# Chunked attention with 64 keys per 32 queries: no mask, a pair of heads in one tile, in front of two MoE layers

## The chip, the core and the metric

The kernel runs on one core of a Trainium2 chip. The metric is the device time of one execution in microseconds (us), as the median of several runs.

## The reference, cut to what matters

```python
batch, n_heads, seq, head_dim, n_mem = 2, 8, 768, 64, 8
chunk, left_ctx, right_ctx = 32, 16, 8
for c in range(seq // chunk):                      # 24 chunks of 32 queries
    l, r = max(0, c*chunk - left_ctx), min(seq, (c+1)*chunk + right_ctx)
    k_full = concat([mem_k, k[:, :, l:r]]); v_full = concat([mem_v, v[:, :, l:r]])   # 8 + up to 56 keys
    a = exp(scores - max(scores)); a = a / (sum(a) + 1e-9)       # scores = q_c @ k_full.T / 8
    out[:, :, c*chunk:(c+1)*chunk] = a @ v_full
x = out as (B, S, 512)
x = sigmoid(xr @ w_r) * (relu(xk @ w_k)**2 @ w_v)  # xk, xr: each row mixed with the row before it
# then: every row goes to one of 8 experts (sticky choice), out = p * (relu(x @ w1[e]) @ w2[e])
```

So each chunk of 32 queries sees at most 8 + 16 + 32 + 8 = 64 keys.

## The kernel before

**Stages.** The 1536 rows are four units of 384 (UT). For a unit, attention runs in 4 pairs of heads, 16 pairs n in all. Its output xT goes through the mixing (`mix_d`, `mix_a`, `mix_hi`, `mix_lo`) into 20 blocks of matmuls per unit: 8 for k (`k_mm`), 4 for r (`r_mm`), 8 halves for v (`v_mm`); a block is 4 triples, and a triple is the three fp32r matmuls of `mm3` (high by high, high by low, low by high part; lines 514 to 516). `v_out` (line 573) ends an output tile. Routing follows (`route_l`, `route_a`, `route_y`, `route_b`, `route_c`), and after the fourth unit come slots of 128 rows for one expert each (`slot_body`) and half slots of 64 rows (`half_body`).

**What sets the order.** The first unit's blocks, the attention of the first two units (pairs 0 to 7) and the preparation of the 20 weight tiles of 128 x 512 (w0 to w19; `w_load`, `w_bias`, three `w_bits`, `w_hi`, `w_lo`, DVE for the most part) stand in one list, `ORDER`, which sets the order on each engine by hand; a negative number chooses a step's second engine. From the second unit on, steps are placed at times of a plan (`at`), 20 of its units per unit of rows, and attention of pairs 8 to 15 lies between the blocks of the second and third unit. PE works through its queue in order.

**Attention before.** A tile of scores is one head g of a pair: 64 queries by 96 keys (8 + 16 + 64 + 8), so that each row holds keys which the chunk must not see. `att_s` first writes a mask into the bank with two bf16 matmuls (lines 359, 360), then adds six products of 64 x 64 x 96 (line 364). `att_max` takes the row maximum on DVE (372, 373), `att_ex` or `att_exp` the exponentials on ACT (389, 379), `att_t` three transposes per head (437), `att_pt` the copy to SBUF. For pairs 0 to 7 `att_pvn` multiplies with V and a column of ones, which gives the sums (402); `att_nm` divides on DVE (410 to 412), `att_xt` transposes the output (418). For pairs 8 to 15 ACT sums while it exponentiates, `att_norm` divides on POOL ahead of the transpose, and `att_pv` gives the output already transposed (453). Scores have banks 2 and 3 in turn, V products bank 5, transposes 4 (and 7), blocks 0 and 1 (and 6 in the first unit), routing 6 and 7.

**The end.** `half_rest` (lines 1222, 1223) walks through nested branches over half slots that no slot took along, then `store` (946) writes the last slot through POOL. Ahead of it, POOL copies the slot's row numbers into `sixl` after each store (1173).

Of the kernel before, what the change touches and what calls it, by code (L numbers as in the profile page):

```python
# [67 lines left out]
)  # L68
BANKS = {"mm": (0, 1), "S": (2, 3), "pt": (4,), "x": (5,), "mi": (6, 7), "mm0": (0, 1, 6), "S0": (2, 3), "pt0": (4, 7)}


def first_unit_steps():
# [3 lines left out]
    room = dict(S=len(BANKS["S0"]), mm=len(BANKS["mm0"]), pt=len(BANKS["pt0"]), x=1, Pm=3, PT=4, tmp=4, dif=2, wcv=3)  # L76
# [5 lines left out]
    for n in range(8):  # L82
        step(f"qk{n}", "load_qk", (n,), [(DMA, 1.4, "")], (n > 5 and f"S{2 * n - 11}", n and f"qk{n - 1}"))
        step(f"v{n}", "load_v", (n,), [(DMA, 1.3, "")], (n > 2 and f"pv{n - 3}", n and f"v{n - 1}"))
    for n in range(8, 11):
        if n < 10:
            step(f"qk{n}", "load_qk", (n,), [(DMA, 1.4, "")], (f"S{2 * n - 11}", f"qk{n - 1}"))
        step(f"v{n}", "load_v", (n,), [(DMA, 1.3, "")], (f"pv{n - 3}", f"v{n - 1}"))
# [10 lines left out]
    for g in range(2 * H):  # L99
        n = g // 2  # L100
        step(f"S{g}", "att_s", (g,), [(PE, 0.8, "")], (f"qk{n}", f"S{g - 1}" if g else "cst"), take="S")
        step(f"mx{g}", "att_max", (g,), [(DVE, 0.65, "")], (f"S{g}",))
        step(f"ex{g}", "att_ex", (g,), [(ACT, 0.72, "")], (f"mx{g}",), take="Pm", give="S")
        step(f"t{g}", "att_t", (g,), [(PE, 0.33, "")], (f"ex{g}",), take="pt", give="Pm")
        step(f"pt{g}", "att_pt", (g,), [(ACT, 0.38, "a"), (DVE, 0.45, "d")], (f"t{g}",), take="PT", give="pt")
        if g % 2:
            step(f"pv{n}", "att_pvn", (n,), [(PE, 0.75, "")], (f"pt{g - 1}", f"pt{g}", f"v{n}", n and f"pv{n - 1}"),
                 take="x", give="PT PT")
            step(f"nm{n}", "att_nm", (n,), [(DVE, 0.85, "")], (f"pv{n}",), take="tmp", give="x")
            step(f"xt{n}", "att_xt", (n,), [(PE, 0.33, "")], (f"nm{n}",), take="pt", give="tmp")  # L110
            step(f"x{n}", "att_xc", (n,), [(ACT, 0.38, "a"), (DVE, 0.45, "d")], (f"xt{n}", n and f"x{n - 1}"), give="pt")
# [37 lines left out]
def kernel(  # L149
# [23 lines left out]
    banks = [psum.tile([P, 512], F32, name=f"bank{i}") for i in range(8)]  # L173
    turn = dict.fromkeys(BANKS, 0)
    spare = {}

    def bank(tag):

        if tag in spare:
            return banks[spare[tag].pop(0)]  # L180
        of = BANKS[tag]
        turn[tag] += 1
        return banks[of[turn[tag] % len(of)]]
# [36 lines left out]
    c_sb = cp.tile([P, 352], F32, name="c_sb")  # L220
# [9 lines left out]
    hi64 = c_sb[:, 136:137]  # L230
    pcol1 = c_sb[:, 158:159]
# [110 lines left out]
    stock["Pm"] = [(ap_.tile([P, NTI, KW], F32, bufs=1, name=f"Pm{k}"), ap_.tile([P, NTI], F32, bufs=1, name=f"sm{k}"))  # L342
                   for k in range(3)]
    stock["PT"] = [ap_.tile([KW, UT], F32, bufs=1, name=f"PT{k}") for k in range(4)]

    def scores(g):
        return Sb[g][:, 0:NTI * KW].rearrange("p (i k) -> p i k", k=KW)

    def att_s(g):
        n, j = divmod(g, 2)  # L350
        Sb[g] = bank("S0" if g < 2 * H else "S")
        s3 = scores(g)


        o = 32 if n // (H // 2) % 2 == 0 else 64
        m = c_sb[o:o + NCK, 192:352].bitcast(BF16)
# [9 lines left out]
        if j == 1 and 8 <= n < NG // 2 - 2:  # L366
            load_qk(n + 2)
# [961 lines left out]
```

## Time and profile before

| what | value |
|---|---|
| three runs | 480.62, 480.97, 481.92 us; median 480.97 |
| profiled execution, its own time | 480.1 us |
| its span, first to last instruction | 478.3 us (1.8 us lie around it) |
| mean granted clock of TensorE | 0.988 of full speed |
| PE busy | 443.8 us, 93% of the span, 3147 matmuls |
| DVE, ACT, POOL busy | 253.8, 201.2 and 108.4 us (53%, 42%, 23%) |

A busy PE need not be at its peak: a matmul's duration in the profile contains its way through the array, and the next one starts before it ends. What PE costs is therefore read below from the distance between starts. The trace records an fp32 matmul as two (two weight loads, two passes); fp32r and bf16 matmuls and transposes are recorded once.

### The profile page before, as it was taken

To read this page: it belongs to the slowest core of one execution; us is meant where nothing else is said; L and a number is where in the kernel's file an instruction comes from. 1 tells how busy PE (TensorE), PEld (TensorE's weight loads), DVE (VectorE), ACT (ScalarE), POOL (GpSimd) and SP (SyncE) were. 2 spreads that over 40 slices of the span, in tenths; PEclk is the share of its full clock that TensorE was granted. 3 is DMA by queue.
4 is the path that set the end of the run, shared out by engine and by line. 5 is a ranking of instruction groups with operands and counts; after the bars stand their busy time and mean duration, and the time that the engine had idled before them with its cause. 6 is when DMAs were issued, how large, how long until landed. Compare 5 with 4: busy or idle time off the path is not lost. (4 is left out here: it accounts for less than half of the span.)

```text
span 478.3 us, 8826 instructions
## 1 busy us (share of the span) xinstructions
PE 443.8 (93%) x3147; PEld 371.0 (78%) x3147; DVE 253.8 (53%) x659; ACT 201.2 (42%) x486; POOL 108.4 (23%) x121
## 2 busy tenths in 40 slices
PE   1898999999999999999999989998999999989990
PEld 1576899989899898999899967785687786757680
DVE  5999997754754448544960287115342115555120
ACT  2666895346442364422470431225342125555220
POOL 2124210114310144100331611310130120214030
PEclk9999999999999999999999999999899999999996
DMA  8998710102222011000192013999650787991020
GB/s 306 350 320 284 284 53 26 51 6 105 68 69 67 26 67 27 0 1 2 44 346 73 0 46 126 383 398 368 234 207 24 284 304 264 407 344 53 23 77 22
DMA packets 27582, 73.46 MB, mean 154 GB/s; under 512 B 3819, under 2 KB 3951, under 8 KB 27520
## 3 DMA queue, kind: packets, MB, share of 16 engines
q1 hardware_dynamic: 24704, 64.23, 38.0%
q0 software_dynamic: 2816, 8.47, 5.2%
q8 instruction: 30, 0.49, 0.4%
q14 instruction: 32, 0.26, 0.2%
HBM read 106.24 MB, written 6.69 MB: 236 GB/s over the span
## 5 line engine op out<-in xcount | busy, mean ns | idle before, releaser
L899 DVE TENSOR_TENSOR w<-bank,w 128x512 fp32r<-128x512 f32 x34 | 23.4, 688 | 73.6 <-ACTq L877 59.3
L514 PE MATMUL bank<-xkh,w 128*128 128x384 f32 x128 | 46.6, 364 | 0.0
L514 PE MATMUL bank<-k2h,w 128*128 128x384 f32 x128 | 44.8, 350 | 0.0
L866 DVE TENSOR_TENSOR w<-raw,w 128x512 fp32r<-128x512 f32 x56 | 35.8, 696 | 16.0 <-ACT w L863 15.6
L516 PE MATMUL bank<-xkh,w 128*128 128x384 f32 x128 | 43.8, 342 | 0.0
L515 PE MATMUL bank<-xkl,w 128*128 128x384 f32 x128 | 43.7, 342 | 0.0
L516 PE MATMUL bank<-k2h,w 128*128 128x384 f32 x128 | 43.0, 336 | 0.0
L515 PE MATMUL bank<-k2l,w 128*128 128x384 f32 x128 | 42.8, 335 | 0.0
L898 ACT ACTIVATE w<-bank 128x512 fp32r<-128x512 f32 x34 | 20.3, 597 | 49.0 <-PE bank L928 27.3
L207 POOL TENSOR_TENSOR k2l<-tmp,k2h 128x384 fp32r<-128x384 f32 x24 | 26.7, 1114 | 51.5 <-DVE k2h L204 29.4
L863 ACT ACTIVATE w<-raw 128x512 fp32r<-128x512 f32 x64 | 35.3, 620 | 4.5 <-DMA raw<-in_w_dram 4.1
L915 PE MATMUL bank<-w,w 128*128 128x512 f32 x88 | 36.1, 411 | 0.5 <-issue 0.5
L937 PE MATMUL bank<-w,w 128*128 128x512 f32 x88 | 36.4, 414 | 0.0
L939 PE MATMUL bank<-w,w 128*128 128x512 f32 x88 | 34.7, 394 | 0.0
L917 PE MATMUL bank<-w,w 128*128 128x512 f32 x88 | 34.5, 392 | 0.0
L916 PE MATMUL bank<-w,w 128*128 128x512 f32 x88 | 34.4, 391 | 0.0
L938 PE MATMUL bank<-w,w 128*128 128x512 f32 x88 | 34.4, 390 | 0.0
L379 ACT ACTIVATE Pm<-bank,mx 128x96 f32<-128x96 f32 x48 | 15.7, 338 | 26.7 <-DVE mx L373 26.7
L514 PEld LDWEIGHTS bank<-xkh,w 128*128 128x128 f32 x128 | 24.5, 191 | 2.8 <-issue 1.9
L364 PE MATMUL bank<-qk 64*64 64x96 f32 x384 | 26.7, 280 | 0.0
L573 DVE SCALAR_TENSOR_TENSOR yT<-yT,bank 128x384 f32<-128x384 f32 x16 | 8.9, 553 | 31.6 <-PE bank L516 31.6
L514 PEld LDWEIGHTS bank<-k2h,w 128*128 128x128 f32 x128 | 24.0, 188 | 0.9
(222 smaller groups left out, 1005.5 us busy)
## 6 DMA issues: line engine op xcount, KB each, us to landing
raw<-in_w_dram SPq DMA_DIRECT2D x36, 2048.0 KB
qk<-in_qkx_dram SPq DMA_DIRECT2D x16, 480.0 KB
vt<-in_vx_dram SPq DMA_DIRECT2D x16, 292.5 KB
w<-in_wk_dram SPq DMA_DIRECT2D x8, 512.0 KB
w<-in_wv_dram SPq DMA_DIRECT2D x8, 512.0 KB
ys<-yr SPq DMA_DIRECT2D x12, 256.0 KB
w<-in_wr_dram SPq DMA_DIRECT2D x4, 512.0 KB
raw<-in_w_dram SPq DMA_DIRECT2D x2, 1024.0 KB
```

The costliest lines, as they stand in the source:

```text
L207: (nc.vector if e == "d" else nc.gpsimd).tensor_tensor(out=o, in0=a, in1=b, op=op)
L514: nc.tensor.matmul(o[:, :UT], lhsT=wh, rhs=xh, start=first, stop=False)
L515: nc.tensor.matmul(o[:, :UT], lhsT=wh, rhs=xl, start=False, stop=False)
L516: nc.tensor.matmul(o[:, :UT], lhsT=wl, rhs=xh, start=False, stop=last)
L863: nc.scalar.activation(out=hi, in_=src, func=ACTF.Copy)
L866: lo_on.tensor_tensor(out=lo, in0=src, in1=hi.bitcast(F32), op=ALU.subtract)
L915: nc.tensor.matmul(pb, lhsT=xh[:, sl], rhs=wh, start=(c == 0), stop=False)
L916: nc.tensor.matmul(pb, lhsT=xh[:, sl], rhs=wl, start=False, stop=False)
L917: nc.tensor.matmul(pb, lhsT=xl[:, sl], rhs=wh, start=False, stop=(c == NC - 1))
L937: nc.tensor.matmul(pb, lhsT=hh[:, sl], rhs=wh, start=(c == 0), stop=False)
L938: nc.tensor.matmul(pb, lhsT=hh[:, sl], rhs=wl, start=False, stop=False)
L939: nc.tensor.matmul(pb, lhsT=hl[:, sl], rhs=wh, start=False, stop=(c == NF - 1))
```

## The change

- Each chunk of 32 queries has a tile of its own: 64 keys, copied by the host into `qkx` and `vx` (KW is 64 instead of 96). No mask remains. Missing keys at the sequence's ends are copies of a memory key with a V row and a ones entry of zero.
- A step handles a pair of heads. `tiles()` yields 24 tiles: three groups of 128 queries, two heads j (their 64 rows of the array), four chunks c (32 columns each). Scores have 24 matmuls of 32 x 64 into two banks (one per head), V products 24 of 32 x 65 into two others.
- One reduction of 384 numbers per row replaces two of 288; there are six exponentials of 64 columns per pair, before six of 96. The two heads' 64 keys stand side by side in the 128 rows of a transpose: three transposes and one copy per pair, before six and two.
- All pairs take the way that pairs 0 to 7 took: sums by the ones column, division on DVE, three transposes of the output.
- Scores have banks 2 and 3 once instead of twice one bank; V products have 5 and 6; blocks of the first unit 0 and 1; routing has 6 and 7 as before, so 6 is shared with the V products.
- `ORDER` is a new list. A tile `qk` has 1152 columns (960), a tile `vt` 128 rows (96).
- At the end one flag (`tab_r`), loaded after the slots, jumps over the whole of `half_rest` when nothing is left for it. The copy into `sixl` moves from POOL, after each store, to DVE, in `put`.

```diff
-KW = NMEM + LCTX + TQ + RCTX
+KW = NMEM + LCTX + CHUNK + RCTX
...
-BANKS = {"mm": (0, 1), "S": (2, 3), "pt": (4,), "x": (5,), "mi": (6, 7), "mm0": (0, 1, 6), "S0": (2, 3), "pt0": (4, 7)}
+BANKS = {"mm": (0, 1), "pt": (4,), "mi": (7,), "mm0": (0, 1), "pt0": (4, 7)}
...
+        if i in (2, 5):
+            two = psum.tile([P, 2, 512], F32, name=f"bank{i}")
+            banks += [two[:, 0], two[:, 1]]
+            Sb, xb = (two, None) if i == 2 else (Sb, two)
...
+    def tiles():
+        for i in range(NTI):
+            for j in range(2):
+                for c in range(P // CHUNK):
+                    yield i, j, i * (P // CHUNK) + c, slice(j * D, (j + 1) * D), slice(c * CHUNK, (c + 1) * CHUNK)
+
+    def att_s(n):
+        for i, j, b, rows, cols in tiles():
+            nc.tensor.matmul(scores[cols, j, i, :], lhsT=qk[n][rows, b * CHUNK:(b + 1) * CHUNK],
+                             rhs=qk[n][rows, UT + b * KW:UT + (b + 1) * KW], start=True, stop=True)
...
+    def att_ex(n):
+        mx = mxs.pop(n)
+        Pm[n] = stock["Pm"].pop(0)
+        for j in range(2):
+            for i in range(NTI):
+                nc.scalar.activation(out=Pm[n][:, i, j, :], in_=scores[:, j, i, :], func=ACTF.Exp, bias=mx[:, j, i:i + 1],
+                                     scale=SCALE)
...
+    def att_pvn(n):
+        for i, j, b, rows, cols in tiles():
+            nc.tensor.matmul(xb[cols, j, i * (D + 1):(i + 1) * (D + 1)], lhsT=PT[n][rows, b * CHUNK:(b + 1) * CHUNK],
+                             rhs=vt[n][rows, b, :], start=True, stop=True)
...
+    def att_t(n):
+        pts[n] = bank("pt0" if n < H else "pt")
+        for i in range(NTI):
+            nc.tensor.transpose(pts[n][:, i * P:(i + 1) * P], Pm[n][:, i].rearrange("p j k -> p (j k)"), ident)
...
+    def att_pair(n, t):
+        at(t, att_s, n)
...
+    banks_of["mi"] = (6, 7)
...
-    half_rest([s >= NMIN for s in HALF_AT].index(True))
+    nr = nc.values_load(ei[0:1, 0, NSLOT + 2:NSLOT + 3], min_val=0, max_val=1)
+    with tc.If(nr):
+        half_rest([s >= NMIN for s in HALF_AT].index(True))
```

How the order moves at three places. PE in the second unit, V products of pair 8 and scores of pair 9 (bank2 and bank5 are the scores' and the products' banks; L621 is a transpose of routing, before L656). Before, the last of twelve V products and the scores of one of the two heads:

```order
L453 MATMUL bank5_69<-PT0_112,vt8_916 64x64
L453 MATMUL bank5_69<-PT2_114,vt8_916 64x64
L359 LDWEIGHTS c_sb_73
L359 MATMUL bank2_66<-c_sb_73 128x192
L360 LDWEIGHTS c_sb_73
L360 MATMUL bank2_66<-c_sb_73 128x96
L364 MATMUL bank2_66<-qk9_603 64x96 x6
```

and after the change the whole of both:

```order
L481 MATMUL bank1_65<-xkh3_114,w7_530 128x384
L388 MATMUL bank5_68<-vt8_970,PT0_106 32x65 x24
L363 MATMUL bank2_66<-qk9_794 32x64 x24
L621 MATMUL bank7_69<-ident_70,r_uk0_1356 8x128 x3
L621 MATMUL bank5_68<-ident_70,r_uk0_1356 8x128 x3
```

A pair's scores now stand in one piece of 24, and the routing's second transpose writes the bank (the second half of bank5) from which DVE divides pair 8.

PE in the first unit where the weight tile w19, the last to be prepared, is first used (k2h7 and k2l7 are the last tiles of its other operand). Before:

```order
L514 MATMUL bank6_70<-k2h7_146,w19_987 128x384
L515 MATMUL bank6_70<-k2l7_147,w19_987 128x384
L516 MATMUL bank6_70<-k2h7_146,w19_987 128x384
L514 MATMUL bank1_65<-k2h6_144,w18_195 128x384
L515 MATMUL bank1_65<-k2l6_145,w18_195 128x384
L516 MATMUL bank1_65<-k2h6_144,w18_195 128x384
L418 MATMUL bank4_68<-ident_72,tmp3_157 128x128 x3
```

and now:

```order
L479 MATMUL bank0_64<-k2h7_138,w19_1078 128x384
L480 MATMUL bank0_64<-k2l7_139,w19_1078 128x384
L481 MATMUL bank0_64<-k2h7_138,w19_1078 128x384
L388 MATMUL bank5_68<-vt6_565,PT0_106 32x65 x24
L479 MATMUL bank1_65<-k2h4_132,w16_1045 128x384
```

From this row to the unit's last block matmul PE had 27 triples, three times three output transposes, one head's transposes and the V products of two pairs; it now has 21 triples, the same output transposes and the V products of two pairs. Ahead of it stood 53 triples and now stand 59, with all scores of pairs 0 to 7 in both.

SP's queue at the last loads of the first unit. Before:

```order
L288 DMA w64_13_626<-in_wv_dram 128x512
L288 DMA w64_3_641<-in_wk_dram 128x512
L266 DMA vt7_676<-in_vx_dram 96x780
L288 DMA w64_17_689<-in_wv_dram 128x512
L288 DMA w64_14_708<-in_wv_dram 128x512
L288 DMA w64_8_729<-in_wr_dram 128x512
L288 DMA w64_19_745<-in_wv_dram 128x512
```

and now:

```order
L260 DMA qk7_681<-in_qkx_dram 128x1152
L293 DMA w64_17_716<-in_wv_dram 128x512
L260 DMA qk8_736<-in_qkx_dram 128x1152
L293 DMA w64_12_753<-in_wv_dram 128x512
L260 DMA qk9_794<-in_qkx_dram 128x1152
L271 DMA vt7_830<-in_vx_dram 128x780
L293 DMA w64_18_848<-in_wv_dram 128x512
```

The tiles of attention are larger, and more of them stand among the last weights.

## Rows read from the trace of the kernel before

**Rows 1.** Windows: engines' busy us, granted clock, DMA share, GB/s by stage.

```profile
5.30:46.00 40.70, 31.43 (x296) 23.41 (x298) 39.44 (x88) 24.97 (x62) 9.83 (x8) 1.00 0.98 331
46.00:80.00 34.00, 33.90 (x289) 30.84 (x288) 32.67 (x72) 27.98 (x71) 5.27 (x5) 1.00 0.42 147
80.00:99.00 19.00, 19.00 (x153) 17.88 (x153) 13.25 (x30) 6.27 (x14) 2.01 (x2) 1.00 0.12 34
99.00:221.00 122.00, 122.00 (x1021) 110.78 (x1021) 65.13 (x210) 50.51 (x170) 29.32 (x33) 1.00 0.14 43
```

**Rows 2.** Timeline about 79 and 99 us: the last weight tile, the first unit's end.

```profile
79.30 0.69 DVE L207 TENSOR_TENSOR w<-wcv,w 128x512 fp32r<-128x512 f32 x1
...
98.81 0.55 DVE L573 SCALAR_TENSOR_TENSOR yT<-yT,bank 128x384 f32<-128x384 f32 x1
```

**Rows 3.** DVE by line, 5.2 to 80 us: count, busy us and mean ns.

```profile
L207 DVE TENSOR_TENSOR w<-wcv,w 128x512 fp32r<-128x512 f32 x17 | 12.6, 747 | 0.5 <-ACT w L202 0.4
L372 DVE TENSOR_REDUCE mx<-bank 128x3 f32<-128x288 f32 x16 | 7.2, 448 | 0.9 <-ACT Pm L389 0.5 <-PE bank L364 0.4
...
L373 DVE TENSOR_SCALAR mx<-mx 128x3 f32<-128x3 f32 x16 | 4.0, 251 | 0.6
L412 DVE TENSOR_TENSOR tmp<-bank,rc 128x384 f32<-128x384 f32 x6 | 3.3, 557 | 0.2
L302 DVE TENSOR_SCALAR wcv<-w 128x512 f32<-128x512 f32 x5 | 2.7, 545 | 4.3 <-DMA w<-in_wk_dram 4.3
```

**Rows 4.** Timeline of PE: one head's scores between two triples (start, length).

```profile
98.27 0.33 PE L515 MATMUL bank<-k2l,w 128*128 128x384 f32 x1
98.44 0.34 PE L516 MATMUL bank<-k2h,w 128*128 128x384 f32 x1
98.71 0.25 PE L359 MATMUL bank<-c_sb 4*128 4x192 bf16 x1
...
98.93 0.71 PE L364 MATMUL bank<-qk 64*64 64x96 f32 x12
99.58 0.44 PE L514 MATMUL bank<-xkh,w 128*128 128x384 f32 x1
```

**Rows 5.** Timeline of PE: a pair's V products between a triple and scores.

```profile
118.33 0.34 PE L516 MATMUL bank<-xkh,w 128*128 128x384 f32 x1
118.60 0.92 PE L453 MATMUL bank<-PT,vt 96*64 96x64 f32 x24
119.45 0.25 PE L359 MATMUL bank<-c_sb 4*128 4x192 bf16 x1
```

**Rows 6.** Timeline of PE: one head's three transposes and what follows.

```profile
115.41 0.49 PE L437 MATMUL bank<-ident,Pm 128*96 128x128 f32 x3
115.74 0.71 PE L656 MATMUL bank<-ident,r_uk 128*8 128x128 f32 x5
```

**Rows 7.** Routing's four products of 32 output rows (route_l): timeline, and durations.

```profile
101.86 0.16 PEld L602 LDWEIGHTS bank<-yT,wg_sb 128*32 128x32 f32 x8 [0.25 <-issue]
101.86 0.85 PE L602 MATMUL bank<-yT,wg_sb 128*32 128x384 f32 x8
...
L602 PE MATMUL bank<-yT,wg_sb x24: 486/498/510, 101.9 to 223.3; 128*32 128x384 f32 x24
```

**Rows 8.** Loads of attention's tiles on SP's queue, KB each.

```profile
qk<-in_qkx_dram SPq DMA_DIRECT2D x16, 480.0 KB
vt<-in_vx_dram SPq DMA_DIRECT2D x16, 292.5 KB
```

**Rows 9.** The end: timeline of the last slot; branches of half_rest (ns min/median/max).

```profile
466.46 0.69 ACT L942 ACTIVATE ot<-bank,yg 128x512 f32<-128x512 f32 x1 [2.16 <-PE bank L939]
472.42 1.02 POOL L946 DMA_INDIRECT out_dram<-ot,sixl  x1 [9.82 <-issue]
...
L1222 PEldq COMPARE_BRANCH  x4: 68/130/4158, 468.0 to 476.3; - x4
...
...
L1223 POOLq INC_SWDGE_SEM  x2: 909/917/925, 467.3 to 468.6; - x2
```

More of the change, by code (lines that the diff above doesn't have):

```diff
@@ L98, in first_unit_steps @@
         step(f"wl{i}", "w_lo", (i,), [(DVE, 0.61, "dl"), (POOL, 1.15, "p")], (f"wh{i}",), give="wcv")
[L99 to L111, printed above, removed]
+    for n in range(H):
+        step(f"S{n}", "att_s", (n,), [(PE, 0.8, "")], (f"qk{n}", n and f"S{n - 1}"), take="S")
+        step(f"mx{n}", "att_max", (n,), [(DVE, 0.75, "")], (f"S{n}",))
+        step(f"ex{n}", "att_ex", (n,), [(ACT, 1.25, "")], (f"mx{n}",), take="Pm", give="S")
+        step(f"t{n}", "att_t", (n,), [(PE, 0.33, "")], (f"ex{n}",), take="pt", give="Pm")
+        step(f"pt{n}", "att_pt", (n,), [(ACT, 0.38, "a"), (DVE, 0.45, "d")], (f"t{n}",), take="PT", give="pt")
+        step(f"pv{n}", "att_pvn", (n,), [(PE, 0.6, "")], (f"pt{n}", f"v{n}", n and f"pv{n - 1}"), take="x", give="PT")
+        step(f"nm{n}", "att_nm", (n,), [(DVE, 0.85, "")], (f"pv{n}",), take="tmp", give="x")
+        step(f"xt{n}", "att_xt", (n,), [(PE, 0.33, "")], (f"nm{n}",), take="pt", give="tmp")
+        step(f"x{n}", "att_xc", (n,), [(ACT, 0.38, "a"), (DVE, 0.45, "d")], (f"xt{n}", n and f"x{n - 1}"), give="pt")
     for n in range(H):
@@ L171 @@
     ys = dram.tile([B * S + 1, YW], F32, name="ys")
-    banks = [psum.tile([P, 512], F32, name=f"bank{i}") for i in range(8)]
+    banks = []
+    for i in range(8):
+        if i in (2, 5):
+            two = psum.tile([P, 2, 512], F32, name=f"bank{i}")
+            banks += [two[:, 0], two[:, 1]]
+            Sb, xb = (two, None) if i == 2 else (Sb, two)
+        elif i not in (3, 6):
+            banks.append(psum.tile([P, 512], F32, name=f"bank{i}"))
     turn = dict.fromkeys(BANKS, 0)
+    banks_of = dict(BANKS)
     spare = {}
@@ L340, in get_xT @@
         return xT[u]
[L342 to L356, printed above, removed]
-        edge, mid = m[:, P:P + KW], m[:, P + KW:P + 2 * KW].unsqueeze(1).to_broadcast([NCK, NTI - 1, KW])
-        ie, im = (slice(0, 1), slice(1, NTI)) if o == 32 else (slice(NTI - 1, NTI), slice(0, NTI - 1))
-        nc.tensor.matmul(s3[:, im, :], lhsT=m[:, 0:P], rhs=mid, start=True, stop=False, skip_group_check=True)
-        nc.tensor.matmul(s3[:, ie, :], lhsT=m[:, 0:P], rhs=edge.unsqueeze(1), start=False, stop=False, skip_group_check=True)
-        x = qk[n][j * D:(j + 1) * D]
-        for b in range(NTU):
-            i, h = divmod(b, 2)
-            nc.tensor.matmul(s3[h * TQ:(h + 1) * TQ, i, :], lhsT=x[:, b * TQ:(b + 1) * TQ],
-                             rhs=x[:, UT + b * KW:UT + (b + 1) * KW], start=False, stop=True, skip_group_check=True)
-        if j == 1 and 8 <= n < NG // 2 - 2:
@@ new lines @@
+    stock["Pm"] = [ap_.tile([P, NTI, 2, KW], F32, bufs=1, name=f"Pm{k}") for k in range(2)]
+    stock["PT"] = [ap_.tile([P, UT], F32, bufs=1, name=f"PT{k}") for k in range(2)]
+    scores = Sb[:, :, 0:NTI * KW].rearrange("p j (i k) -> p j i k", k=KW)
+    def tiles():
[7 more added lines that the diff above has]
+                             rhs=qk[n][rows, UT + b * KW:UT + (b + 1) * KW], start=True, stop=True)
+        if 8 <= n < NPR - 2:
@@ L385, in att_ex @@
-    def att_ex(g):
-        mx, s3 = mxs.pop(g), scores(g)
-        Pm[g], sm[g] = stock["Pm"].pop(0)
-        for i in range(NTI):
-            nc.scalar.activation(out=Pm[g][:, i, :], in_=s3[:, i, :], func=ACTF.Exp, bias=mx[:, i:i + 1], scale=SCALE)
-        leave("S0", Sb[g])
-        del Sb[g]
+    def att_ex(n):
[5 more added lines that the diff above has]
+                                     scale=SCALE)
@@ L393 @@
     xn = {}
     def att_pvn(n):
-        xb[n] = bank("x")
-        for i in range(NTI):
-            for j in range(2):
-                for h in range(2):
-                    b = 2 * i + h
-                    o = (2 * i + j) * (D + 1)
-                    nc.tensor.matmul(xb[n][h * TQ:(h + 1) * TQ, o:o + D + 1], lhsT=PT[2 * n + j][:, b * TQ:(b + 1) * TQ],
-                                     rhs=vt[n][:, b, j, :], start=True, stop=True)
-        stock["PT"] += [PT.pop(2 * n), PT.pop(2 * n + 1)]
@@ L415, in att_xt, with att_pt @@
+    def att_t(n):
+        pts[n] = bank("pt0" if n < H else "pt")
+        for i in range(NTI):
+            nc.tensor.transpose(pts[n][:, i * P:(i + 1) * P], Pm[n][:, i].rearrange("p j k -> p (j k)"), ident)
+        stock["Pm"].append(Pm.pop(n))
+    def att_pt(n, e="a"):
+        PT[n] = stock["PT"].pop(0)
+        copy(e, PT[n], pts[n][:, :UT])
+        if n < H:
+            leave("pt0", pts[n])
+        del pts[n]
     def att_xt(n):
-        pts[n, "x"] = bank("pt0")
+        pts[n, "x"] = bank("pt0" if n < H else "pt")
@@ L727 @@
         if u > 1:
-            for i in range(H):
-                att_group(u * H + i, T - 20 + 2.0 * i, 1.0)
+            for i in range(H // 2):
+                att_pair(u * H // 2 + i, T - 19 + 4.0 * i)
             for c in range(NC):
@@ L942, in put @@
         nc.scalar.activation(out=ot[0], in_=banks[2 + s % 2], func=ACTF.Copy, scale=yg[s % 3][:, DM:DM + 1])
+        nc.vector.tensor_copy(sixl, six[:, s:s + 1])
     def store():
@@ L1155 @@
     put(0)
-    nc.gpsimd.tensor_copy(sixl, six[:, 0:1])
     nv = nc.values_load(ei[0:1, 0, NSLOT:NSLOT + 1], min_val=0, max_val=NFULL)
@@ L1172, in slot_body @@
         store()
-        nc.gpsimd.tensor_copy(sixl, six[:, s:s + 1])
         gather(s + 2)
```

177 lines of the change are left out of this document (66 added, 111 removed), and 37 rows, old and new, of the table ORDER.

## The prediction, made before the changed kernel ran

> **What bounds the kernel now.** I read the stages first, then the engine that is full in each, then single pieces in the timeline. The windows [rows 1] show two regimes. From 5.3 to 80 us DVE is busy 72.1 of 74.7 us (39.44 + 32.67): it prepares the 20 weight tiles, takes row maxima and divides. The loads are nearly as full in the first part of it (share 0.98 to 46 us). PE is full from 46 us on. The last weight tile, w19, is ready at 80.0 us (79.30 + 0.69), and 18.8 us later DVE's last product of the first unit begins, at 98.81 [rows 2]: DVE decides when w19 comes, PE how long the rest takes. From 99 to 221 us, the second and third unit, PE is busy all the time and DVE for 65.1 us of 122 [rows 1]: whatever PE is spared there comes off the end. The fourth unit and the slots hold no attention. Their work and waits hang on each other and not on absolute time, so they should move forward as a whole.
>
> What attention costs PE is the distance between starts. An ordinary triple member takes 0.17 us (98.27 to 98.44), a triple 0.52. One head's scores take 98.44 to 99.58, 1.14 us less the 0.17 that the next start takes anyway: 0.97, of which the masks 0.22 (98.71 to 98.93) [rows 4]. A pair's V products take 118.33 to 119.45 less 0.17, 0.95 us, of which 0.68 are the 24 recorded passes (0.85 to the next piece less 0.17) and 0.27 the way in and out [rows 5]. Three transposes take 0.33 [rows 6]. A pair of units 3 and 4 of rows, which run inside the 99 to 221 window, therefore costs PE 2 x 0.97 + 0.95 + 2 x 0.33 = 3.55 us.
>
> **The price that the trace doesn't show.** Scores and V products become 24 matmuls each, 48 passes of 64 or 65 columns, in tiles of 64 rows by 32 columns. No such tile ran before. The nearest row is routing's product with 32 output rows [rows 7]: eight passes of 384 columns have 0.85 us in all, 0.50 of that the last one's own length, so 0.35 us from the first start to the last. One behind the other at 0.17 each they would need 1.2. Four lay side by side. If four do so here, 48 passes of 64 columns take as long as 24 passes two by two did: 0.68, with the way in and out 0.95 us, for the scores as for the V products. The bounds: 0.61 if both heads' rows also run side by side (half of 0.68, and 0.27), 2.99 if nothing does (0.68 / 24 x 2 = 0.057 per pass, 48 of them, and 0.27). I take 0.95, the row nearest in shape.
>
> The tiling page speaks for the low end. The Trainium skill ("TensorEngine Tiling (Array Packing)", Available Configurations and Gotcha 1) lists 64 x 32 as eight independent tiles and asks that row tiles write different banks, as the two heads' scores do here. By it scores and V products would take 0.61 us each.
>
> **Term 1, first unit, -7.9 us.** DVE up to w19, counted in the two orders with the durations of [rows 3]: 16 maxima of 0.448 + 0.251 become 8. The reduction of 384 numbers lies between 0.448 and 0.747 (the 512 wide operation); I take 0.557, the 384 wide one that reads a bank: -4.7. `w_bias` moves to ACT in three cases (-1.6), one subtraction of a weight to POOL (-0.7), one division of a pair now stands behind w19 (-0.9), and small moves of mixing steps from POOL and ACT to DVE give back 1.7. Together -6.2 of durations; since neighbouring instructions overlap, the 81 us of durations in that stretch filled 72.1 us, and it is worth 0.89 x 6.2 = 5.5. w19 is ready at 74.5. PE has to have done its work in front of it by then: 59 triples, eight pairs' scores, their transposes, six V products and five output transposes, 30.7 + 7.6 + 4.3 + 5.7 = 48.3 us in the 65 us since the start: covered. From w19 on PE had 27 triples, four sets of transposes and two V products, 14.0 + 1.3 + 1.9 = 17.2 us, and now has 21, three and two: 13.8. That is -3.4. Against it: the tiles of attention grow from 480 and 292.5 KB [rows 8] by a fifth and a third (1152 columns for 960, 128 rows for 96). Ten qk and eight vt stand ahead of the last weight, together 1.78 MB, 5.4 us at the 331 GB/s of a full stretch [rows 1]. Most of it lies beside DVE's work, since w18, the last load, is wanted only some 66 us in. I count 1 us late (bounds 0 and 5.4). -5.5 - 3.4 + 1 = -7.9.
>
> **Term 2, second and third unit, -6.9 us.** Pairs 8 to 15 cost 2 x 0.95 + 2 x 0.33 = 2.56 us (the output's transposes are new here), before 3.55: -0.99 each, -7.9 in all. The division, 0.557 and two small operations per pair, comes to DVE, which is idle for 57 of 122 us, and POOL and ACT lose work. Against it: routing's second transpose writes the bank that DVE has still to read for the pair just before it in PE's queue; the next blocks stand behind it. Scores of the next pair and one transpose, 1.3 us, cover a division of about 0.9. I count 0.5 us per unit (bounds 0 and 1), 1 in all. That the scores have no second set of banks costs nothing: 16 triples, 8.3 us, lie between one pair's scores and the next.
>
> **Term 3, the end, -2 us.** The last slot's output is ready at 467.15 (466.46 + 0.69), its store starts at 472.42: POOL spends the time in skipped branches, among them two of 0.92 us at line 1223, and PE's branches run to 476.3, with one of 4.16 [rows 9]. One skip remains, plus the loading of a flag. The nearest bounds are 0 and 4; I take 2. The copy into `sixl` on DVE is free, for the store before is long done.
>
> **Sum.** The profiled execution took 480.1 us, 478.3 of span and 1.8 around it. 480.1 - 7.9 - 6.9 - 2 = 463.3. The median of the three runs, 480.97, lies 0.9 above that execution; I leave the difference out.
>
> **Rivals.** *A, eight tiles side by side.* For it speaks that the heads' rows are apart; nothing in the trace shows row tiles together. Each of the 16 pieces of pairs 8 to 15 saves another 0.34, and the two V products behind w19 too: -5.4 - 0.7, 457.2 us.
>
> *B, passes cost what they cost two by two,* 0.028 us each, because small passes are limited by their issue and not by their columns. Then a piece takes 48 x 0.028 + 0.27 = 1.63: +0.68 for 16 pieces, 10.9, two more behind w19, 1.4, and the work in front of w19 rises to 57.8 us, with little cover left, 1: 476.6 us. Against it: the eight weight loads of [rows 7], 0.106 us and more each, lie within 0.16 us, so issue is not the limit there. The Trainium skill ("TensorE: Matmul & The Clock Gate", Wait, 56ns, not 53.3ns?) gives a floor of about 25 ns from start to start, however small the matmul. By that rule a piece would take 1.47 us and the kernel about 473; the loads of [rows 7] lie closer together than that.
>
> *C, slower: tiles of 64 x 32 do not overlap at all.* A piece takes 2.99 us. Pairs 8 to 15 get 32.6 us worse than my forecast, the V products behind w19 4.1, and the work in front of w19 becomes 76.9 us where 65 are there, 11.4: 511 us. It decides from 0.034 us per pass: there the 18 pieces eat the whole 16.8 us. Against it stand the rows with two and with four side by side.
>
> *D, the loads become the bound of the first unit.* They are at 0.98 already, and all 5.4 us end up in w19's time: 467.7 us. Against it: after 46 us their share falls to 0.42, so there is room behind.
>
> **How the numbers follow.** My forecast 0.56, A 0.14, D 0.11, B 0.10, C 0.06, and 0.03 for smaller shifts of the kind of D and A. 463.3 is the likeliest; its own range is 458 to 468 (the reduction's price 2, the loads 1 more, the end 2 either way). To take in A and D the range goes from 453 to 471 and leaves out B and C, 0.16. What a measurement of this kernel can tell from no change is about 0.3%, 1.4 us. Faster by more: all but C and a third of B, where the loads or waits add to it: 0.91. Within it: that part of B, 0.03. Slower: C, 0.06.
>
> **What will show it.** The timeline of a score piece: 0.95 us from the triple before to the triple after (less 0.17), 0.61 for A, 1.63 for B. DVE's last weight subtraction ends at 75 us, or at 80 for D, with DVE waiting for loads. The last `v_out` of the first unit starts near 91. The second and third unit take 115 us, not 122. The last store starts about 2 us earlier with respect to the last output. I am wrong if the clock of PE stays at its lower level for long in the first unit, whose PE work becomes thinner, or if a wait for the routing's shared bank shows in the second and third unit.

## The result, and the profile after

The changed kernel takes 460.43 us (median of four runs, 459.79 to 462.49); in the same comparison the kernel before took 480.8 us. The ratio is 0.9593, 95% interval 0.954 to 0.9645: 4.1% faster. The forecast was 463.3 us, its range 453 to 471. The profiled execution took 459.8 us, its span 458.0.

```profile
span 458.0 us, 10040 instructions
PE 414.9 (91%) x3827; PEld 351.1 (77%) x3827; DVE 251.0 (55%) x628; ACT 187.3 (41%) x425; POOL 94.2 (21%) x96
```

PE has more instructions (3827 matmuls, before 3147) and 29 us less to do; DVE has 3 us less.

I cut both spans at the same events: the last `v_out` of each unit, the beginning of the last output on ACT (`put`), the end.

| stretch | before | after | difference | forecast |
|---|---|---|---|---|
| to the first unit's last `v_out` | 98.81 | 92.56 | -6.25 | -7.9 |
| second and third unit | 122.11 | 111.89 | -10.22 | -6.9 |
| fourth unit and slots | 245.54 | 245.39 | -0.15 | 0 |
| last output to the end | 11.86 | 8.12 | -3.74 | -2 |
| span | 478.3 | 458.0 | -20.3 | -16.8 |

Each of the three terms is there, none has its size. The windows of the changed kernel answer to [rows 1]. The columns are, as there, PE, PEld, DVE, ACT and POOL, granted clock, DMA share, GB/s; the stretches are cut where PE's unbroken work begins and where the first and the third unit end:

```profile
5.30:45.40 40.10, 21.55 (x480) 16.98 (x480) 37.94 (x77) 22.49 (x58) 7.97 (x7) 1.00 0.93 352
45.40:92.60 47.20, 47.06 (x594) 43.55 (x602) 44.30 (x92) 33.15 (x82) 10.05 (x10) 1.00 0.43 156
92.60:204.50 111.90, 109.72 (x1374) 102.96 (x1364) 63.58 (x186) 40.47 (x114) 17.46 (x17) 1.00 0.17 55
```

Until 45.4 us PE works little more than half of the time and DVE nearly all of it; then PE is full to the end of the unit, with DVE only a little less full beside it.

The granted clock of the first row, 1.00, doesn't fit the starts on PE: triple members stand 0.32 us apart until 42.2 us and 0.173 from there. In `e5_relief` (below), whose first triples on PE are 0.32 us apart as well, the same view has 0.50 there, the lower of the clock's two levels (1.2 of 2.4 GHz):

```profile
36.00:42.00 6.00, 4.86 (x15) 4.46 (x16) 6.00 (x12) 2.57 (x6) 1.56 (x2) 0.50 0.92 342
```

So a spacing of 0.32 is read below as the lower level and 0.173 as the higher.

**Prices on PE.** The timeline of PE shows V products alone (start, length):

```profile
78.92 0.34 PE L481 MATMUL bank<-k2h,w 128*128 128x384 f32 x1
79.19 0.73 PE L388 MATMUL bank<-vt,PT 64*32 64x65 f32 x48
79.85 0.45 PE L479 MATMUL bank<-k2h,w 128*128 128x384 f32 x1
```

From triple to triple 0.93 us, less the 0.17 that the next start takes anyway: 0.76. The seven undivided pieces behind 45 us give 0.75 each, scores or V products. Where the next pair's scores stand right behind, both together take 1.23 (107.10 to 108.50, less 0.17; the six such couples 1.22 to 1.28):

```profile
107.10 0.34 PE L481 MATMUL bank<-xkh,w 128*128 128x384 f32 x1
107.36 0.67 PE L388 MATMUL bank<-vt,PT 64*32 64x65 f32 x44
...
107.88 0.68 PE L363 MATMUL bank<-qk 64*32 64x64 f32 x44
108.50 0.49 PE L621 MATMUL bank<-ident,r_uk 128*8 128x128 f32 x3
109.99 0.49 PE L621 MATMUL bank<-ident,r_uk 128*8 128x128 f32 x3 [1.00 <-DVE tmp L400]
```

The forecast had 0.95 and, for both, 1.90. The last row is the wait for the shared bank: from one `L621` to the next piece of three 1.49 us lie where 0.33 would do (the distance in `e3_route`, where nothing is waited for), and the one waited for is `L400`, the division of the pair just before.

A pass is one recorded matmul; an fp32 product of a tile has two. The starts of the 48 passes of the piece at 79.19 us, worked out of the trace as distances in ns, tell how they share the array:

```
7 7 6 7 7 6 7 | 34 7 7 6 7 7 6 7 | 10 6 7 7 6 7 7 6 | 10 7 7 6 7 7 6 7 | 27 57 8 17 17 16 17 12 | 5 11 5 12 17 16 17 17
```

Eight passes start 7 ns apart; 82 ns after the first the second eight begin, 57 ns later the third: eight tiles run side by side. Behind some 32 passes it is over. The last 16 come mostly 17 or 12 and 5 ns apart, the loads of their weights likewise. On the mean it is 10.9 ns per pass (0.51 us from the first start to the last), and 10.4 to 10.8 where 96 passes stand together.

### The profile page after: what moved, and what is told of

It reads as the page before. It is cut to its first block, busy times and chain, and to the rows that moved or that the text cites. A ratio compares the mean times of both kernels' runs of the same rounds, so it can differ in the third digit from the quotient of the medians.

```text
span 458.0 us, 10040 instructions
## 1 busy us (share of the span) xinstructions
PE 414.9 (91%) x3827; PEld 351.1 (77%) x3827; DVE 251.0 (55%) x628; ACT 187.3 (41%) x425; POOL 94.2 (21%) x96
## 5 line engine op out<-in xcount | busy, mean ns | idle before, releaser
L863 ACT ACTIVATE w<-bank 128x512 fp32r<-128x512 f32 x34 | 20.3, 597 | 54.3 <-PE bank L893 32.7
L381 ACT ACTIVATE Pm<-bank,mx 128x64 f32<-128x64 f32 x96 | 21.3, 322 | 21.8 <-DVE mx L372 21.3
L505 ACT ACTIVATE tmp<-bank 128x384 f32<-128x384 f32 x24 | 11.9, 494 | 41.5 <-PE bank L481 38.8
L479 PEld LDWEIGHTS bank<-xkh,w 128*128 128x128 f32 x128 | 24.8, 194 | 4.4 <-issue 1.9
L480 PEld LDWEIGHTS bank<-xkl,w 128*128 128x128 f32 x128 | 24.8, 194 | 1.4 <-DVE xkl L211 1.4
L481 PEld LDWEIGHTS bank<-xkh,w 128*128 128x128 f32 x128 | 24.7, 193 | 0.0
```

The costliest lines, as they stand in the source:

```text
L479: nc.tensor.matmul(o[:, :UT], lhsT=wh, rhs=xh, start=first, stop=False)
L480: nc.tensor.matmul(o[:, :UT], lhsT=wh, rhs=xl, start=False, stop=False)
L481: nc.tensor.matmul(o[:, :UT], lhsT=wl, rhs=xh, start=False, stop=last)
```

## The experiments

Twelve kernels ran, all of them the changed kernel with one, two or three edits, or none. The slots, to which no edit belongs, took between 195.6 and 199.0 us in their profiles (196.1 in the changed kernel): a difference of a microsecond or two is therefore read from the places in the trace, not from the whole time. Part of it is PE's clock. The five profiles with the longest slots (197.3 to 199.0 us) show the lower level for 3 to 7 us in or behind a wait of PE that ends at 320 to 326 us, the others (195.6 to 196.7) don't. In `e2_cols`, the longest:

```profile
322.00:328.00 6.00, 5.73 (x24) 2.83 (x26) 1.70 (x5) 0.60 (x2) 0.00 (x0) 0.50 0.33 82
```

### Four tiles or eight: `e1_rows`

```diff
     def tiles():
-        for i in range(NTI):
-            for j in range(2):
+        for j in range(2):
+            for i in range(NTI):
```

> Scores and V products walk through one head's 64 rows completely (12 matmuls) before the other's, so that only four tiles of 64 x 32 follow one another, no longer eight; all results stay the same. In the changed kernel a piece of 48 passes alone takes 0.75 us (start to start, less 0.17), V products with the next scores behind them 1.23. Theory 1 (eight tiles run side by side, and a tile takes 57 ns from one pass to the next): now four passes start every 57 ns, the 48 need 0.64 us from first start to last (0.51 before), a piece 0.89 us, two behind each other 1.55 to 1.6; six such couples and four single pieces in the second and third unit, +2.7 us there, +0.5 to 1 in the first unit, 463.5 to 464.5 us in all. Theory 2 (a pass costs its 10.6 ns whichever tile it goes to, because something in front of the array hands them out): pieces stay at 0.75 and 1.23, the time at 460.4. Theory 3 (the forecast's price, four side by side in the changed kernel already): no change either.

Measured: 462.36 us (460.64 to 463.04), ratio 0.9668 (0.9619 to 0.9716). The V products, from the timeline of PE:

```profile
79.07 0.34 PE L481 MATMUL bank<-k2h,w 128*128 128x384 f32 x1
79.34 0.78 PE L388 MATMUL bank<-vt,PT 64*32 64x65 f32 x48
80.04 0.45 PE L479 MATMUL bank<-k2h,w 128*128 128x384 f32 x1
```

A piece costs 0.80 us (0.97 - 0.17), two together 1.34; first start to last 0.558 and 1.097. Every piece has got dearer, so that theories 2 and 3 fall as they stand; but by 0.05 and not by the 0.14 of theory 1. Its 0.64 counted twelve fours one behind the other, 57 ns apart. The starts of the piece at 79.34 show that only at first: fours begin at 0, 81, 137, 163 and 194 ns, and 26 or 31 ns are less than the 57 after which a tile got its next pass in the changed kernel. From there passes of both heads seem to run together here too; the trace doesn't name the tile. The couple with and without the alternation, 1.34 and 1.23, gives what alternating is worth, 0.11 us. What the second row half is worth in itself this run doesn't show, since it was at work in both. The second and third unit take 0.4 and 0.25 us more by it (56.54 and 55.97, in the changed kernel 56.16 and 55.72).

### What a pass costs: `e2_cols`

```diff
+            w = KW if b == NCH - 1 else 2 * KW
-            nc.tensor.matmul(scores[cols, j, i, :], lhsT=qk[n][rows, b * CHUNK:(b + 1) * CHUNK],
-                             rhs=qk[n][rows, UT + b * KW:UT + (b + 1) * KW], start=True, stop=True)
+            nc.tensor.matmul(wide[cols, j, i, 0:w], lhsT=qk[n][rows, b * CHUNK:(b + 1) * CHUNK],
+                             rhs=qk[n][rows, UT + b * KW:UT + b * KW + w], start=True, stop=True)
```

`wide` is the same bank with 128 columns per group, `scores` its first 64.

> Each score matmul (but for the last chunk of a unit) multiplies 128 columns of keys where 64 are wanted; the second 64 land in a part of the bank that nobody reads, all results stay the same. V products are untouched and serve as the measure beside it (0.51 us from first start to last of 48 passes, 0.75 the piece). Theory 1 (eight tiles side by side, and two limits: the columns for the first 24 passes or so, the handing out of passes, 10 to 17 ns each, for the rest): the columns now take 8 passes every 110 ns, 48 in 0.59 to 0.65 us from first start to last, the piece 0.83 to 0.9. Theory 2 (handing out alone): scores stay at 0.51 and 0.75. Four tiles side by side would need 1.2 us from first start to last. The whole kernel: +1 to 1.5 us by theory 1, 460.4 by theory 2, +10 with four side by side.

Measured, one run: 465.1 us. Scores in the timeline:

```profile
55.55 0.34 PE L483 MATMUL bank<-xkh,w 128*128 128x384 f32 x1
55.82 0.92 PE L365 MATMUL bank<-qk 64*32 64x128 f32 x48
56.67 0.44 PE L481 MATMUL bank<-xkh,w 128*128 128x384 f32 x1
```

The piece costs 0.95 us, 0.65 from first start to last; the untouched V products stay at 0.75 and 0.51. Theory 1 has the distances right (0.59 to 0.65) and the piece slightly low, since the way out grows as well. Eights of 128 columns follow one another at 109 ns, where those of 64 need 57, so the columns set the pace of the first passes; but twice the columns make the piece only 0.14 longer than 0.51, so with 64 columns they are not what limits the whole of it. (Of the 5.3 us by which its span is longer 2.9 lie in the slots, where the clock fell; the second and third unit have 1.2 and 0.9, more than theory 1 said, as the wait for the shared bank grew too.)

### The shared bank: `e3_route`, `e8_route2`, `e9_route3`

Only two numbers of the plan change, the places `bt` of `route_b` and `ct` of `route_c` in the second and third unit; the diff is that of `e3_route`, `e8_route2` has (5.5, 9.02), `e9_route3` (5.5, 8.02):

```diff
-            yt, bt, ct = ((2.02, 3.02, 4.02), 5.02, 7.02) if u < NU - 2 else ((3.02, 4.02, 5.02), 2.02, 3.52)
+            yt, bt, ct = ((2.02, 3.02, 4.02), 5.5, 7.02) if u < NU - 2 else ((3.02, 4.02, 5.02), 2.02, 3.52)
```

> Only the place of route_b in the plan of the second and third unit changes (5.5 for 5.02): a block of four triples now lies between the V products and routing's transposes, the second of which writes the bank that DVE divides from. Theory 1 (the wait of 1.27 us from one L621 to the next is the shared bank): it goes, each of the two units gets 1.1 us shorter, 458.2 us. Rival (the division is late for another reason, or the work behind routing waits in its place): a wait of the same length shows in front of another piece, 460.4 us.

> As the run with route_b a block later, and route_c two blocks later (9.02 for 7.02), since it waited 2.5 us for the scans there. Theory: neither the shared bank nor the scans are waited for now, both units lose 1.1 us, 458.2 us. Rival (something behind routing needs the rows in time, or the steps of pairs on DVE come later behind the scans): 460.4 or more.

> route_b at 5.5 and route_c at 8.02 of the plan: the transposes of routing have a block between them and the V products, route_c comes 2 us later than in the changed kernel (when the scans are done) and a whole block ahead of the next V products. Theory (the shared bank costs 1.1 to 1.2 us in each of the two units, and the two runs before only met other waits: the scans at 7.02, the next division from the shared bank at 9.02): second and third unit take 55.1 and 54.6 us (56.16 and 55.72 in the changed kernel), 458.2 us in all. Rival (every place behind 5.02 costs something of its own): 56 us or more each, 460.4 us or more.

Measured: 466.67 us (465.62 to 467.15), 463.25 (463.09 to 464.83) and 463.38 (461.57 to 465.6). In all three the transposes of `route_b` run through without a wait, as the theory has it: that wait was the shared bank. But each time `route_c` (`L653`, from the timelines of PE of the three runs in this order) waits in its place:

```profile
115.11 0.34 PE L480 MATMUL bank<-xkl,w 128*128 128x384 f32 x1
117.67 0.84 PE L653 MATMUL bank<-c_sb,r_ukt 8*128 8x16 f32 x6 [2.21 <-DVE r_ukt L630]
```

```profile
119.52 0.45 PE L479 MATMUL bank<-xrh,w 128*128 128x384 f32 x1
121.31 0.84 PE L653 MATMUL bank<-c_sb,r_ukt 8*128 8x16 f32 x6 [1.34 <-DVE tmp L400]
```

```profile
117.64 0.84 PE L653 MATMUL bank<-c_sb,r_ukt 8*128 8x16 f32 x6 [1.20 <-DVE r_ukt L630]
```

At 7.02 and 8.02 it waits for the scans (`L630` ends them), which on DVE now come behind a cast that itself waits for ACT; at 9.02 it stands behind the next V products and waits for the division from the shared bank once more. The second and third unit take 59.1 and 58.5, 56.5 and 57.5, 56.4 and 57.2 us, more than the 56.2 and 55.7 of the changed kernel. Part of that is the clock: behind these waits of 1.2 to 2.2 us it fell to its lower level for 3.4 us in both units of `e3_route` and in the third unit of the other two, which costs PE up to half of that each time. The first time in `e3_route`:

```profile
118.70:122.00 3.30, 3.30 (x13) 3.20 (x13) 2.34 (x13) 1.39 (x3) 0.32 (x1) 0.50 0.05 0
```

The second unit of `e8_route2` and `e9_route3` had no such fall and took 56.5 and 56.4; `e10` below, with the places of `e9_route3` and no fall, has 56.41 and 55.84. So the rivals were right that nothing is gained (`e3_route` lost 6 us, where its rival had none): of the places tried 5.02 is the cheapest, and the 1.2 us per unit were not to be had this way.

### The end: `e4_tail`

```diff
-    nr = nc.values_load(ei[0:1, 0, NSLOT + 2:NSLOT + 3], min_val=0, max_val=1)
-    with tc.If(nr):
-        half_rest([s >= NMIN for s in HALF_AT].index(True))
+    half_rest([s >= NMIN for s in HALF_AT].index(True))
```

> Only the flag that jumps over half_rest is taken out; the copy into sixl stays on DVE. In the changed kernel the last output is ready at 450.53 and the last store starts 2.30 us later, before the change 5.27 us; from that output's start to the end of the span it is 8.16 us, before 11.84. Theory 1 (the nested branches are what the store waited for): the store starts 5.0 to 5.3 us after the output, the time is 463.4 to 464.1 us. Rival (the copy on POOL was part of it, the flag brings less): the store starts 3 to 4 us after the output, 461 to 462.5 us.

Measured: 462.89 us (462.59 to 464.58). The end of the changed kernel, which answers to [rows 9] (last output, last store), and below it that of this run:

```profile
449.84 0.69 ACT L907 ACTIVATE ot<-bank,yg 128x512 f32<-128x512 f32 x1 [2.16 <-PE bank L904]
452.83 1.02 POOL L912 DMA_INDIRECT out_dram<-ot,sixl  x1 [9.36 <-ACTq L1188]
```

```profile
450.18 0.69 ACT L907 ACTIVATE ot<-bank,yg 128x512 f32<-128x512 f32 x1 [2.16 <-PE bank L904]
453.76 1.02 POOL L912 DMA_INDIRECT out_dram<-ot,sixl  x1 [9.93 <-ACTq L1194]
```

From the output's beginning to the end of the span it is 8.12 us in the changed kernel, 11.12 here, 11.86 before the change: without the flag it is 3.0 longer. In the other eleven profiles with the flag this stretch takes 8.11 to 8.93, so the flag is worth between 2.2 and 3.0, and the remaining 0.7 to the kernel before is no more than that spread: what the copy that moved from POOL to DVE brings to the end is not shown. The store itself comes only 0.6 us later without the flag (2.89 us behind the finished output, with it 2.30), where before it was 5.27: theory 1 misses the store clearly, and the rival's store (3 to 4 us) is just missed; the time lies between the two theories', nearer to the rival's. Most of what the flag saves lies behind the store: 7.54 us from its start to the end, with the flag 5.13.

### What decides the first unit: `e5_relief`, `e6_warm`, `e7_pool`

`e5_relief`:

```diff
         elif k == 1:
+            if i >= 15:
+                return
```

> Leaves out one of the three bit operations (0.60 us each) for the last five weight tiles, all of them behind 64 us of the first unit: the weights are wrong, and with them everything behind, so only the first unit's times are read: when w19 is ready (78.07 us in the changed kernel) and when the unit's last v_out starts (92.56). Theory P (behind 45.4 us PE is the limit: it is busy without a wait and reaches w19's triple at 78.58, after w19): w19 is ready at 75.1, the last v_out stays at 92.3 to 92.6. Theory D (w19's time sets the end, as in the forecast): the last v_out comes 3 us earlier, 89.6.

`e6_warm` (the numbers of `WARM` are steps of `ORDER`, behind which so many matmuls follow):

```diff
+WARM = {169: 6, 178: 12, 185: 4, 187: 5, 194: 4, 200: 4, 198: 7}
...
             F[fn](*args, *([e] if len(on) > 1 else []))
+            for _ in range(WARM.get(abs(k), 0)):
+                nc.tensor.matmul(banks[0][:, 0:256], lhsT=ib[:, 0:P], rhs=ib, start=True, stop=True)
```

> Adds 42 bf16 matmuls of 128 x 128 by 256 columns to PE in the gaps between 16 and 38 us (into bank 0, which nobody uses by then, read by nobody); all results stay the same. In the changed kernel triples are 0.32 us apart until 42.2 us and 0.173 from there, in the kernel before the change the spacing of 0.173 begins earlier. Theory P (PE's thinner work kept the lower clock longer, and what follows 45.4 us is PE's alone): the clock rises before 36 us, PE's unbroken work begins 1.5 to 2.5 us earlier, but w19 at 78.07 now comes before PE is free for it only by little, so that the unit's last v_out moves to 92.0 to 92.3 only, the time to 460. Rival D (DVE alone decides): the clock rises, w19 and the last v_out stay within 0.1. Rival C (clock unaffected by so few matmuls): spacing changes at 42 us as before.

`e7_pool` turns the sign of nine steps of `ORDER` (58, 236, 44, 242, 79, 249, 299, 100, 264), as here the first, and puts 236 behind 63 and 100 behind 121:

```diff
-    174, -58, -60, 175
+    174, 58, -60, 175
```

> Moves POOL's nine steps before 78 us of the first unit (four subtractions of weights, two differences, two low parts of the mix, one of k2) to DVE, near the same places of the list. In the changed kernel eight DVE instructions that ran while POOL worked took 0.5 to 1.1 us longer than their kind, 5.7 us in all, in the kernel before the change 3.0 us. Theory S (the two engines take turns, DVE pays nearly all that POOL works): DVE gets 4.9 us of work, loses the 5.7 us and a wait of 0.7, and w19 is ready at 76.5 to 77. Rival (the long instructions have another reason, and go on): w19 is ready at 82 to 83, the last v_out at 96 to 97, 464 us.

The changed kernel, DVE's last weight subtraction (w19) and the unit's last `v_out`:

```profile
77.39 0.68 DVE L211 TENSOR_TENSOR w<-wcv,w 128x512 fp32r<-128x512 f32 x1
92.56 0.56 DVE L538 SCALAR_TENSOR_TENSOR yT<-yT,bank 128x384 f32<-128x384 f32 x1 [1.53 <-PE bank L481]
```

The same two in `e5_relief`, and below in `e7_pool`:

```profile
76.28 0.68 DVE L211 TENSOR_TENSOR w<-wcv,w 128x512 fp32r<-128x512 f32 x1
92.58 0.56 DVE L540 SCALAR_TENSOR_TENSOR yT<-yT,bank 128x384 f32<-128x384 f32 x1 [1.53 <-PE bank L483]
```

```profile
75.36 0.69 DVE L211 TENSOR_TENSOR w<-wcv,w 128x512 fp32r<-128x512 f32 x1
91.19 0.55 DVE L538 SCALAR_TENSOR_TENSOR yT<-yT,bank 128x384 f32<-128x384 f32 x1 [1.53 <-PE bank L481]
```

`e5_relief`: w19 is ready 1.1 us earlier (not 3; DVE now meets other waits), and the unit ends where it did. Theory D falls. Behind 45 us w19's time does not set the end, though in the changed kernel it is ready only 0.5 us before PE takes it (78.07 and 78.58).

`e6_warm`, 462.05 us: the spacing of 0.173 begins at 38.9 us, with the first triples (granted clock 1.00 from 25.3 to 45.7 us), but PE then waits 1.94 us for ACT, starts at 45.72, not 45.45, and has spacings of 0.32 again for three microseconds (from 46.20; granted clock 0.50 there); the last `v_out` comes at 93.79. None of the three had it: rival C is out, the clock did rise early; but the added matmuls also delayed V products, and with them DVE's divisions (w19 is ready at 79.3), so that the run doesn't tell theory P from D on the clock. `e11` below does.

`e7_pool`, 459.16 us (458.25 to 460.28): w19 0.5 us earlier than theory S said, the rival is out. One of the long DVE instructions of the changed kernel, with what POOL did meanwhile (its kind takes 0.68):

```profile
49.08 1.38 POOL L211 TENSOR_TENSOR k2l<-tmp,k2h 128x384 fp32r<-128x384 f32 x1 [11.59 <-ACT k2h L206]
49.51 1.50 DVE L317 SCALAR_TENSOR_TENSOR wcv<-w,wcv 128x512 uint32<-128x512 uint32 x1
```

It ends 0.55 us after POOL's, as if it had done little before. Without POOL's work there is no long one left before 78 us: the 5.7 us (3.0 before the change) were DVE waiting for POOL. The Trainium skill ("SBUF — State Buffer", SBUF: two separate sides) calls the pair of ports that both engines share an exclusive lock, held for the whole instruction. The trace agrees: six of the long DVE instructions end 0.28 to 0.55 us after POOL's, somewhat less than their own length without POOL (0.42 to 0.69).

The unit gets 1.37 us shorter because PE's unbroken work begins 1.26 us earlier, at 44.19. What it waits for is seen in the timelines of DVE, ACT and PE of the changed kernel:

```profile
43.64 1.27 DVE L211 TENSOR_TENSOR w<-wcv,w 128x512 fp32r<-128x512 f32 x2
44.35 0.67 ACT L305 ACTIVATE wcv<-w 128x512 f32<-128x512 f32 x1 [0.78 <-DVE w L211]
44.92 0.47 ACT L499 ACTIVATE tmp<-bank 128x384 f32<-128x384 f32 x1
45.45 0.44 PE L479 MATMUL bank<-xkh,w 128*128 128x384 f32 x1 [0.92 <-ACT tmp L499]
```

ACT's `w_bias` waits until DVE's subtraction gives back a buffer; the ReLU that empties PE's bank stands behind it in ACT's queue; PE, which has only banks 0 and 1 for blocks, waits for that.

### Together, and once more: `e10_pool_route3`, `e11_pool_route3_warm`, `e12_again`

`e10` joins the edits of `e7_pool` and `e9_route3`; `e12` is the changed kernel itself; `e11` adds to `e10` the matmuls of `e6_warm` at two places only:

```diff
-WARM = {169: 6, 178: 12, 185: 4, 187: 5, 194: 4, 200: 4, 198: 7}
+WARM = {200: 4, 198: 7}
```

> Both edits together: POOL's nine steps of the first unit on DVE (alone: the last v_out of the first unit at 91.19 for 92.56), and routing's places 5.5 and 8.02. They lie in different stages, so the gains should add: first unit 91.2, second and third 55.1 and 54.6, 456.9 us. Rival (they share something): 458 or more.

> As the run with both edits, and 11 bf16 matmuls (read by nobody) in PE's last two gaps of the first unit, behind the scores of pair 4 and behind the output transposes of pair 3, where nothing of DVE's hangs on PE (the 42 in the run before delayed the V products and with them the divisions). Theory (the first triples at 0.32 us cost what follows): spacing of 0.173 from 38 us on, the unbroken work begins about 1 us earlier, the last v_out of the first unit at 90.2 to 90.6, 456 us. Rival (DVE alone sets the beginning, a higher clock only makes the gap behind it longer): the last v_out stays at 91.1 to 91.3, 456.9 us.

> The changed kernel unaltered, on the same chip as the three variants above, for a comparison that takes no detour over the kernel before: 460.4 us, between 459.5 and 462.5 in every run.

Measured: 460.47 us (459.58 to 462.91), 461.31 (460.29 to 463.13) and 460.99 (459.49 to 462.02). `e10` ends the first unit at 91.36, which repeats `e7_pool`, and loses 0.4 us in the next two (56.41 and 55.84), as `e9_route3` did with more; in time it cannot be told from the changed kernel. In `e11` the matmuls bring the higher clock earlier (spacing 0.173 from 37.6 us, in `e10` from 42.1), and in this unit it buys nothing:

```profile
42.18 0.34 PE L482 MATMUL bank<-xkh,w 128*128 128x384 f32 x1
44.46 0.44 PE L480 MATMUL bank<-xkh,w 128*128 128x384 f32 x1 [1.95 <-ACT tmp L500]
```

The triples ahead of the wait are over at 42.18 (43.32 in `e10`), the wait is as much longer, and the unbroken work begins at 44.46 (44.39 in `e10`), the last `v_out` at 91.46. The rival was right: DVE, through ACT, sets that beginning, whatever PE's clock was. (Its second unit takes 57.66, with a granted clock of 0.51 from 118.7 to 122.0, behind a wait of 1.21 us.)

No version was shown to be faster than the changed kernel. `e7_pool` alone is 1.4 us ahead in the trace and had the lowest median, but it was not timed against the changed kernel on one chip, and the ranges overlap.

## Why the forecast was right in its sign and range, and where its steps were off

**The price of a piece** (0.95 us for scores and for V products alike) was mis-sized: it measured 0.75 alone and 1.23 for both together. The step took "four side by side" and 24 passes' time for 48. Rival A's mechanism, eight tiles side by side, is there for the first 32 passes (eight per 57 ns are the 7 ns per pass that its 0.61 us means), and its 1.22 for the two pieces is close to the 1.23 of a couple, but not for its reason: a piece alone is 0.75 and not 0.61, because the last 16 passes take 0.27 us, longer than the first 32 (0.24); what a couple gains over two pieces alone, it gains where they meet. Limits are the columns for the first passes and 10 to 17 ns per pass for the rest (`e2_cols`). What hands passes out so slowly was not tested. The 10.9 ns per pass refute B (28) and C (57), and 0.75 us is half of the 1.47 that stands under B as well. (C's own sum is slightly off: 76.9 less 65 is 11.9, not 11.4; nothing else rests on it.)

**Term 2, -6.9, measured -10.2.** The mechanism held, its two prices did not. I added up the distances between starts by line, and to a piece what the triple members just before and behind it need above 0.17 (the way in, and a first member of 0.28 us). So the attention of four pairs costs 8.53 us in the second unit and 8.23 in the third, 2.10 per pair; before 14.58 and 14.26, 3.61 per pair (forecast, without that first member, 2.56 and 3.55). That is -1.51 per pair and not -0.99, 4.2 more for eight pairs. The shared bank, named as a sign of being wrong, was waited for: 1.2 per unit, not 0.5, and above the bound of 1: +1.3. Routing's other pieces got 0.15 per unit cheaper. -6.9 - 4.2 + 1.3 - 0.3 = -10.1.

**Term 1, -7.9, measured -6.25: the wrong step.** "DVE decides when w19 comes, PE how long the rest takes" is refuted for the changed kernel by `e5_relief`. PE was busy without a gap from 45.15 us on before the change as well, which [rows 1] already showed (33.90 of 34.00 us); I called the 48.3 us in front of w19 covered by 65 us since the start, but PE can't use most of the first 40 of them: in the changed kernel it waits 10.5 us for the first loads, then 8.5 for DVE and 4.9 for ACT. The unit is DVE's until 45 us and PE's from there. PE's last wait in the unit before the change:

```profile
45.15 0.55 PE L418 MATMUL bank<-ident,tmp 128*128 128x128 f32 x3 [0.49 <-DVE tmp L412]
```

PE's part went from 53.66 us (45.15 to 98.81) to 47.11 (45.45 to 92.56), -6.55, and of that attention's pieces are 15.1 - 8.9 = 6.2; the beginning moved by +0.30. Up to there DVE's row maxima fell from 6.8 to 3.4 us, but the new order puts 17 mixing steps ahead (11.7 us) where 7 stood before (4.1), and fewer steps of weights; how much each moved the beginning was not tested, only that the waits for POOL are a part (`e7_pool`, 1.26 earlier without them). w19 itself was ready at 78.07 and not at 74.5; of these 3.6 us 2.7 are, by their lengths, the longer waits for POOL (5.7 us for 3.0), for which the forecast had no term. The reduction's price itself was right, 0.546 us for the 0.557 taken:

```profile
L371 DVE TENSOR_REDUCE mx<-bank 128x6 f32<-128x384 f32 x8 | 4.4, 546 | 0.0
```

**The loads** (1 us, rival D 5.4): nothing. Behind its start DVE waits for no load in the unit; D did not happen. **The clock**, named as what could make me wrong: triples 0.32 us apart lasted until 42.2 us (in the kernel before, a head's scores are down from 1.00 to 0.71 us by 37.9), and `e11` shows that it costs nothing there.

**Term 3, -2, measured -3.7**, inside its bounds of 0 and 4: of it the flag 2.2 to 3.0; whether the copy that I had called free has a part in the rest is not shown. PE's branches still take long with the flag, one of 4.29 us:

```profile
L1203 POOLq INC_SWDGE_SEM  x1: 908/908/908, 449.1 to 449.1; - x1
L1203 PEldq COMPARE_BRANCH  x1: 4293/4293/4293, 451.1 to 451.1; - x1
```

The three errors (+1.65, -3.3, -1.7) leave 3.4 us in the sum, since one of them has the other sign. That 463.3 came within 0.6% of 460.43 is in part luck.

## What to carry to other kernels

A stage with one full engine is that engine's from where its gaps end, even if another engine, nearly as full, finishes something late in it: look for the last gap first, and ask what ended it. In pieces like these, small tiles of the array ran side by side for the first few dozen passes only; after that count passes, not columns, and put pieces next to each other so that they share the way in and out. A wait that disappears when a step is moved says what it waited for, not that the time can be had: the step's followers wait next.

## What the runs showed of the hardware that I had not expected

- In tiles of 64 rows by 32 columns passes start 7 ns apart in groups of eight, then, behind some 32 passes, 17 or 12 and 5 ns apart, in every single piece looked at (0.51 us for 48; 0.985 to 1.03 for 96 in a couple).
- A DVE instruction that meets one of POOL's takes up to 1.1 us longer; moving nine POOL steps (1.0 to 1.7 us each) onto DVE made DVE's last weight 2.0 us earlier, although DVE then had more to do.
- A skipped branch lasted 4.29 us on PE and 0.91 on POOL at the end of the program.
- The slots, with the same instructions, took 195.6 to 199.0 us in different executions of kernels that differ only ahead of them, and the longer ones are those in which PE's clock fell on the way. From 42 us to the last output each fall to the lower level came in a wait of PE of 1.2 to 2.7 us or at most 2.1 us behind it, but waits as long went by without one (1.95 us before 44.46 us in `e11`, 2.8 before 320 us in the changed kernel).
